# A gated attention unit and its feed-forward layer: staging buffers given to scores, fewer interleaved up groups, respaced score units

## The chip, the cores and the metric

The kernel runs on one core of a Trainium2 chip. A core has five engines with queues of their own: TensorE (PE, matmuls; its weight loads are listed apart as PEld), VectorE (DVE), ScalarE (ACT), GpSimd (POOL) and SyncE (SP, which here only issues transfers). Transfers between main memory and the core's SBUF, and transposing transfers inside SBUF, run on 16 DMA engines; SP, ACT and POOL issue them. Matmul results land in PSUM, eight banks of 128 x 512 f32. The metric is the device time of one execution in microseconds (us); less is better.

## The reference

```python
def _attn_ref(u, v, z):                       # u, v: 8 x 3008 x 256, z: 8 x 3008 x 64
    scores = (1.0 / S) * np.matmul(z, z.transpose(0, 2, 1))
    attn = np.maximum(scores, 0.0) ** 2
    return u * np.matmul(attn, v)

def _moe_ref(x, w_in, w_out):                 # x: 24064 x 256, w_in: 256 x 2048, w_out: 2048 x 256
    h = x @ w_in
    g = h * (1.0 / (1.0 + np.exp(-1.702 * h)))
    return g @ w_out
```

Eight batches of attention with a squared relu in place of a softmax, gated by u, and a feed-forward layer over all rows. The scores are symmetric: the block of rows i and columns j is the transpose of block (j, i).

## The kernel before

**Tiles.** Each batch has 24 row blocks of 128 rows (the last half full) in six chunks of 512 rows (`NCH` = 6, `NJ` = 24). A *score unit* (i, jp) is two row blocks (2jp, 2jp + 1) against chunk i: two score matmuls in 64-row halves of TensorE that run together into a PSUM tile `sc` of two banks (tag "ps2", two tiles, shared with the up-projection's `hg`), a relu by ACT into `rl` (three buffers) and a square by VectorE into `a`. The buffers of tag "a" (21 of them, 2 KB a partition each) hold these units, and also the left sums S1, S2, S4 described below. Because of the symmetry, most units serve a second chunk as well: SP transposes them by a transfer into tiles `tt` (tag "tt", 15 buffers of 4 KB), a tag that the activated tiles `gt` of the feed-forward layer and the staging of the first batch's V and z use too. In batches after the first, the unit on the diagonal is "folded": unit (i, 2i) is computed whole, (i, 2i + 1) only in part, and the rest of it, tile `ad`, comes from a transposing transfer; VectorE writes the other half of `ad`.

**The loop.** The body loops over batches b and chunks i. `attend(b, i)` returns some 47 steps of two matmuls (0.216 us of TensorE each; 0.189 in chunk 5, which is 448 wide) that multiply V by the units into `o` (tag "ps1", four banks). Every engine's order is the order of the program text. Between the steps the loop inserts other work at step numbers written out by hand: score units at the steps in `SCHED0`, `SCHED`, `NEXT` (a dictionary from step to number of units, `take` pops them from a queue in a fixed order), transposes of u (`TURN`), loads (`LOAD`, `LOADW`), and in chunk 4 of a batch (`full(b)`; chunk 5 in the last batch) the *heads*: the first `LAGY` = 18 up groups, spread evenly over the steps. In chunk 5 the inserted units are those of the next batch's chunk 0 (`host` = b + 1); two more are taken at the end of the batch.

**The feed-forward layer.** A batch has 48 up groups q (`up_group`): six blocks k of 512 rows, eight groups each. A group is four matmuls into `hg`, a gelu by ACT into `gf` (two buffers), and a scaled copy to `gt` by VectorE (by ACT where q is at least `LAGY` and q % 4 = 1). The second matmul is done for blocks 0 to 4 (0 to 5 in odd batches) in Strassen's way, with seven products P1 to P7 instead of eight: `left_sums` computes S1 to S4 from a block's `gt` on VectorE, two operations each, and `weight_sums` computes t1 to t4 from W2 once. These operations stand in the list `SUMS`; each up group pops one (two while the list is longer than eight), and a block's eight sums are appended after its last up group. After chunk 5 a loop runs over the remaining up groups, each followed by one product from the list `products`: for k = 0 P1, P6, P5, P7, P2, then for each next k P1(k), P4(k-1), P3(k-1), P6(k), P5(k), P7(k), P2(k), and at the end P4, P3 of the last. Each product is 16 matmuls, 0.89 us. Products that are left behind the last up group are run as `steps`, each of which pops one sum. P6 reads S2 and t2, P5 S1 and t1, P7 S3 and t3, P3 S4, P4 t4. Results go to `y` (tag "y", two buffers) by operations on ACT (`uP`, `y`) and VectorE (`y`), which stand in the engines' queues where their product stands. In even batches block 5 (384 rows) goes through plain matmuls (`down`).

**The first batch's start.** z comes by SP and ACT, is cast by `first_cast` (groups 0 to 3 by VectorE, 4 and 5 by ACT) and transposed by TensorE. V comes in six loads of 512 KB in f32 (`load_v`: two by ACT, four by SP) into staging tiles of tag "tt", and POOL casts each with two copies. In later batches V is loaded by POOL with a cast in the transfer, and z by `load_z` through two staging tiles `zst`.

The lines that the prediction's steps touch: L232 score matmul, L246 and L243 relu, L260, L251 and L244 squares (`a`, half `ad`), L253 and L272 transposing transfers, L332 the attention matmul, L349 to L352 the gate, L373 up matmul, L381 gelu, L383 and L385 `gt`, L420 to L423 weight sums, L441 to L449 left sums, L474 products, L484 to L490 their results.

Of the kernel before, what the change touches and what calls it, by code (L numbers as in the profile page):

```python
# [9 lines left out]
F32 = mybir.dt.float32  # L10
F16 = mybir.dt.float16
P = 128
# [3 lines left out]
def kernel(  # L16
# [13 lines left out]
    AF = mybir.ActivationFunctionType  # L30
    ALU = mybir.AluOpType

    B, S, D = u.shape
    DQK = z.shape[2]
    DFF = moe_w_in.shape[1]

    NJ = (S + P - 1) // P
# [61 lines left out]
    def first_z(n0, n1, eng):  # L99

        if 0 not in ZT:
            ZT[0] = pz.tile([P, NJ, P], F16, name="ZT", tag="ZT")
            ZT["st"] = [pa.tile([P, CB * CB, 2, DQK], F16, name="zst", tag="tt", bufs=15) for _ in range(2)]
            ZT["f"] = [pw.tile([P, CB * CB, DQK], F32, name="zf", tag="y") for _ in range(2)]
        zf = ZT["f"][n0 // (CB * CB)]
        m0 = n0 % (CB * CB)
        t0, last = n0 * P, n1 == NJ
        t1 = (n1 - CB if last else n1) * P
        eng.dma_start(
            zf[:, m0:m0 + (t1 - t0) // P, :].rearrange("p (g n) d -> p g (n d)", n=CB),  # L110
            z[0, t0:t1].rearrange("(g p n) d -> p g (n d)", p=P, n=CB),
        )
        if last:
            m1 = m0 + (t1 - t0) // P
            eng.dma_start(zf[:, m1:m1 + CB - 1, :], z[0, t1:S0].rearrange("(p n) d -> p n d", n=CB - 1))
            for h in range(2):
                eng.dma_start(zf[h * SREM:(h + 1) * SREM, m1 + CB - 1, :], z[0, S0:S])

    def first_cast(g, by_act=False):
        m = g % CB * CB  # L120
        for c in range(2):
            dst, src = ZT["st"][g // CB][:, m:m + CB, c, :], ZT["f"][g // CB][:, m:m + CB, :]
            if by_act:
                act.activation(dst, src, AF.Copy, scale=1.0)
            else:
                dve.tensor_copy(dst, src)

    def first_zt(g):

# [20 lines left out]
    def load_z(b):  # L150
        ZT[b] = pz.tile([P, NJ, P], F16, name="ZT", tag="ZT")
        for n0 in range(0, NJ, NU):
            zst = pu.tile([P, NU, 2, DQK], F16, name="zst", tag="zst")
            full = min(NU, NJ - 1 - n0)
            src = z[b, n0 * P:(n0 + full) * P].rearrange("(n p) d -> p n d", p=P)
            pool.dma_start(zst[:, :full, 0, :], src)
            if full < NU:
                for h in range(2):
                    pool.dma_start(zst[h * SREM:(h + 1) * SREM, full, 0, :], z[b, S0:S])
            pool.tensor_copy(zst[:, :, 1, :], zst[:, :, 0, :])  # L160
            sp.dma_start_transpose(ZT[b][:, n0:n0 + NU], zst.rearrange("p n c d -> p (n c d)"))
# [5 lines left out]
    def load_v(b, n0):  # L167

        if n0 == 0:
            V16[b] = pz.tile([P, NJ, D], F16, name="V16", tag="V16")  # L170
        if b:
            dst, eng = V16[b][:, n0:n0 + VB], pool
        else:
            dst, eng = pa.tile([P, VB, D], F32, name="vst", tag="tt", bufs=15), act if n0 < 2 * VB else sp
        full = min(VB, NJ - 1 - n0)
        eng.dma_start(dst[:, :full, :], v[b, n0 * P:(n0 + full) * P].rearrange("(n p) c -> p n c", p=P))
        if full < VB:
            for h in range(2):
                eng.dma_start(dst[h * SREM:(h + 1) * SREM, full, :], v[b, S0:S])
        if b == 0:  # L180
            for n in range(0, VB, 2):
                pool.tensor_copy(V16[b][:, n0 + n:n0 + n + 2], dst[:, n:n + 2])

# [55 lines left out]
    def square(b, i, jp, sc):  # L239
        rl = pw.tile([P, 2, CH], F16, name="rl", tag="rl", bufs=3)  # L240
        if folded(b, i) and jp == 2 * i + 1:
            rh = rl[:, :, :CH // 2]
            act.activation(rh, sc[:, :, :CH // 2], AF.Relu, scale=csc)  # L243
            dve.tensor_tensor(unit[b, i, jp][:, 1], rh, rh, ALU.mult)  # L244
            return
        act.activation(rl, sc, AF.Relu, scale=csc)  # L246
        if folded(b, i) and jp == 2 * i:
            a = pa.tile([P, CB, 2, P], F16, name="a", tag="a", bufs=21)
            unit[b, i, jp] = a
            r4 = rl.rearrange("p r (q c) -> p r q c", q=CB)  # L250
            dve.tensor_tensor(a.rearrange("p q r c -> p r q c"), r4, r4, ALU.mult)  # L251
            unit[b, i, jp + 1] = pa.tile([P, 2, 2, CH // 2], F16, name="ad", tag="a", bufs=21)
            sp.dma_start_transpose(  # L253
                unit[b, i, jp + 1][:, 0].rearrange("p g (r c) -> p (g r) c", c=P),
                a[:, CB // 2:].rearrange("p q r c -> p (q r c)"),
            )
            return
        a = pa.tile([P, 2, CH], F16, name="a", tag="a", bufs=21)
        unit[b, i, jp] = a
        dve.tensor_tensor(a, rl, rl, ALU.mult)  # L260
        if jp // 2 > i and (turned(b, i) or jp < NU - 2):
            if b and i == 0 and LATE:
                late.append(((jp + 2) % NU, lambda: turn_unit(b, i, jp, a)))
            else:
                turn_unit(b, i, jp, a)

    def turn_unit(b, i, jp, a):
        cj = jp // 2
        if (b, i, cj) not in TT:
            TT[b, i, cj] = pa.tile([P, CB, CB, P], F16, name="tt", tag="tt", bufs=15)  # L270
        k0 = 2 * (jp % 2)
        sp.dma_start_transpose(  # L272
            TT[b, i, cj][:, k0:k0 + 2].rearrange("p r g c -> p (r g) c"),
            a.rearrange("p r c -> p (r c)"),
        )
# [90 lines left out]
    def up_group(b, q):  # L366
        k, fg = divmod(q, NFG)
        i, n = blocks(b)[k]
        hg = ps2.tile([P, FFG, CH], F32, name="hg", tag="ps2")
        for e in range(FFG):  # L370
            ff = fg * FFG + e
            for c in range(NCC):
                pe.matmul(  # L373
                    hg[:, e, :n], W1[:, c, ff * P:(ff + 1) * P], XT[b, i][:, c, :n],
                    start=(c == 0), stop=(c == NCC - 1),
                )
        if fg % 2 == 0:
            GT[b, k, fg // 2] = pa.tile([P, CB, CH], F16, name="gt", tag="tt", bufs=15)
        g = GT[b, k, fg // 2][:, (fg % 2) * FFG:(fg % 2 + 1) * FFG, :n]
        gf = pw.tile([P, FFG, CH], F32, name="gf", tag="gf")  # L380
        act.activation(gf[:, :, :n], hg[:, :, :n], AF.Gelu_apprx_sigmoid, scale=1.0 / FSC)  # L381
        if q >= LAGY and q % 4 == 1:
            act.activation(g, gf[:, :, :n], AF.Copy, scale=FSC)  # L383
        else:
            dve.tensor_scalar(g, gf[:, :, :n], FSC, None, ALU.mult)  # L385
        for s_ in [SUMS.pop(0) for _ in range(min(len(SUMS), 1 + (len(SUMS) > 8)))]:
            s_()
        if k < nst(b) and fg == NFG - 1:
            SUMS.extend(left_sums(b, k) + (weight_sums() if b == k == 0 else []))

# [44 lines left out]
    def left_sum(b, k, name, h):  # L437
        a11, a12, a21, a22 = left(b, k, h, 0), left(b, k, h + 2, 0), left(b, k, h, 1), left(b, k, h + 2, 1)
        if name == "S3":
            ST[b, k, name, h] = a21  # L440
            dve.tensor_tensor(a21, a11, a21, ALU.subtract)  # L441
            return
        s_ = ST[b, k, name, h] = pa.tile([P, CB, 2, P], F16, name="s", tag="a", bufs=21)
        if name == "S1":
            dve.tensor_tensor(s_, a21, a22, ALU.add)  # L445
        elif name == "S2":
            dve.tensor_tensor(s_, ST[b, k, "S1", h], a11, ALU.subtract)  # L447
        else:
            dve.tensor_tensor(s_, a12, ST[b, k, "S2", h], ALU.subtract)  # L449
# [89 lines left out]
        if last:  # L539
            store(b, k, pool)  # L540

    LAGY = 2 * NFG + 2
    HEAD = 2

    def pieces(b, i):
# [6 lines left out]
        k = max(len(lst) - 6, 2)  # L552
        return lst[:k] + lst[-2:] + lst[k:-2]

    NEXT = {n: 1 for n in (3, 8, 13, 17, 31, 36, 41, 46)} | {NJ: 2}
    SCHED = {
        0: {n: 1 for n in (3, 7, 11, 15, 19, 29, 33, 37, 41, 45)} | {NJ: 2},
        1: {n: 1 for n in (2, 7, 12, 17)} | {NJ: 2},
        2: {n: 1 for n in (2, 7, 12, 17)} | {NJ: 2},
        3: {n: 1 for n in (6, 14, 32, 38)} | {NJ: 2},  # L560
        4: {},
# [35 lines left out]
        load_v(0, n0)  # L597
    first_z(2 * CB, 4 * CB, sp)
    first_z(4 * CB, NJ, sp)
    for n0 in range(2 * VB, NJ, VB):  # L600
        load_v(0, n0)
    warm_up(7)
    for g in range(2):
# [14 lines left out]
    for b in range(B):  # L618
# [5 lines left out]
        for i in range(NCH):  # L624
# [4 lines left out]
            for n, step in enumerate(attend(b, i, b == 0 and i < 2)):  # L629
# [2 lines left out]
                if b == 0 and i == 0 and n == 3:  # L632
                    turns[1]()
                if b == 0 and i == 0 and n in FIRST_CAST:
                    first_cast(FIRST_CAST[n], True)
                if b == 0 and i == 0 and n in FIRST_ZT:
                    first_zt(FIRST_ZT[n])()
                if (i, n) in turn:
# [8 lines left out]
                if i == full(b) and n >= HEAD and (n - HEAD) * LAGY // (2 * NJ - 10) >= head and head < LAGY:  # L647
                    up_group(b, head)
                    head += 1
                step()  # L650
        late.sort(key=lambda t: t[0])
        if more:
            for i in range(2):
# [58 lines left out]
```

## Time and profile before

| | us |
|---|---|
| median of six runs | 1203.72 |
| lowest and highest | 1199.45, 1206.33 |
| the profiled execution | 1204.03 |
| its span, first to last instruction | 1202.3 |

| engine | busy us | share |
|---|---|---|
| PE | 1186.3 | 99% |
| ACT | 825.5 | 69% |
| DVE | 823.4 | 68% |
| POOL | 234.6 | 20% |

The profile gives each instruction's start and duration, the idle time of its engine before it, and what ended that idle time (`<-`). Names read out<-in. In the timeline a line is: start, duration (from the first start to the last end of the merged group), engine, line, operation, tiles, shapes, number of instructions, idle time before. In the list of waits it is: total us, times, longest. In the table of stretches: length, then busy us and instructions of PE, PEld, DVE, ACT, POOL, then the granted clock, the share of the 16 DMA engines and GB/s. Matmuls overlap: one of 128 x 512 is listed with some 0.38 us, while the next starts after 0.216. The granted TensorE clock is 0.999 over the span; it is 0.91 in the stretch from 40 to 60 us. A batch takes some 148 us: batch 1 begins at 166.6, its chunk 4 ends near 240, its chunk 5 near 252, and its last product at 315.4.

### The profile page before, as it was taken

The numbers are of one execution on the slowest core, as the hardware profiler recorded it, in microseconds if no ns is written. First come the engines' busy times: TensorE is split into PE (matmuls) and PEld (weight loads), VectorE is DVE, ScalarE is ACT, GpSimd is POOL, SyncE is SP. The second block draws the span as 40 slices with busy tenths as digits, with TensorE's granted clock in tenths as the row PEclk, the third lists the DMA queues.
The fourth block names the chain that finished last, engine by engine and source line by source line (L and its number), as shares of the span: only waits on it lengthen the run. The fifth ranks groups of instructions, "written<-read, shape, count | busy, mean of one in ns | idle before, by whom it ended". The sixth has DMA issues, their size and how long they took to land.

```text
span 1202.3 us, 27542 instructions
## 1 busy us (share of the span) xinstructions
PE 1186.3 (99%) x11427; PEld 724.5 (60%) x11427; DVE 823.4 (68%) x1323; ACT 825.5 (69%) x979; POOL 234.6 (20%) x325
## 2 busy tenths in 40 slices
PE   8999999999999999999999999999999999999998
PEld 3345775467754676546765468554775547855577
DVE  6688855778657775577775777547786577654776
ACT  7787864678656786477864787657776578672785
POOL 5143100331002310123101231013210132101000
PEclk9999999999999999999999999999999999999999
DMA  9996567676587767757778478784688846785012
GB/s 219 178 129 105 130 141 132 90 116 129 122 139 84 119 129 144 128 64 119 133 148 133 57 119 151 146 120 71 98 150 155 117 77 96 163 158 101 1 36 72
DMA packets 373022, 141.81 MB, mean 118 GB/s; under 512 B 315424, under 2 KB 366368, under 8 KB 372896
## 3 DMA queue, kind: packets, MB, share of 16 engines
q1 hardware_dynamic: 314256, 96.77, 44.2%
q0 software_dynamic: 57280, 42.03, 23.7%
q8 instruction: 89, 1.46, 0.5%
q10 hardware_dynamic: 1360, 1.25, 0.3%
q14 instruction: 37, 0.30, 0.1%
HBM read 60.29 MB, written 24.64 MB: 71 GB/s over the span
## 4 chain that ended last, share of the span: by engine, by line
PE 92%; DVE 3%; ACT 3%; DMA 2%; issue 1%; SPq 0%; DVEq 0%; ACTq 0%
PE o L332 36%; PE hg L373 25%; PE st L474 23%; PE sc L232 6%; PE yp L530 2%; ACT rl L246 2%; DVE gt L385 1%; ACT gf L381 1%; DMA tt<-a 1%; DMA zf<-in_z_dram 1%; DMA vst<-in_v_dram 0%; DVE ut L201 0%; DVE s L445 0%; DVE a L260 0%; DVE s L447 0%
## 5 line engine op out<-in xcount | busy, mean ns | idle before, releaser
L381 ACT ACTIVATE gf<-hg 128x1024 f32<-128x1024 f32 (+1 forms) x384 | 385.9, 1005 | 135.1 <-PE hg L373 111.4
L246 ACT ACTIVATE rl<-sc 128x1024 f16<-128x1024 f32 x309 | 304.5, 1025 | 157.8 <-PE sc L232 144.8
L332 PEld LDWEIGHTS <-V 64*128 64x128 f16 (+1 forms) x4052 | 241.0, 95 | 236.8 <-issue 13.6
L373 PE MATMUL hg<-xt,W 128*128 128x512 f16 (+1 forms) x1408 | 354.6, 374 | 0.8 <-ACT gf L381 0.6
L385 DVE TENSOR_SCALAR gt<-gf 128x1024 f16<-128x1024 f32 (+1 forms) x328 | 229.4, 699 | 128.0 <-ACT gf L381 126.6
L332 PE MATMUL o<-a,V 64*128 64x512 f16 (+3 forms) x2286 | 304.2, 369 | 0.0
L260 DVE TENSOR_TENSOR a<-rl 128x1024 f16<-128x1024 f16 x274 | 187.9, 694 | 155.2 <-ACT rl L246 149.7
L194 POOL DMA_DIRECT2D uq<-in_u_dram x188 | 126.7, 681 | 622.0 <-PE sc L232 268.9
L332 PE MATMUL o<-tt,V 64*128 64x512 f16 (+1 forms) x1510 | 237.2, 378 | 2.5 <-DMA tt<-a 2.5
L373 PEld LDWEIGHTS <-W 128*128 128x128 f16 x1536 | 139.9, 98 | 125.2 <-issue 5.8
L474 PEld LDWEIGHTS <-gt 128*128 128x128 f16 x2816 | 169.2, 98 | 30.4
L474 PEld LDWEIGHTS <-s 128*128 128x128 f16 x2112 | 127.2, 98 | 22.8
L232 PE MATMUL sc<-ZT 64*128 64x512 f16 (+1 forms) x688 | 122.0, 367 | 6.9 <-ACT rl L246 6.0
L474 PE MATMUL st<-WT,gt 128*128 128x128 f16 x1408 | 93.0, 219 | 0.0
L474 PE MATMUL st<-W,gt 128*128 128x128 f16 x1408 | 92.3, 219 | 0.0
L474 PE MATMUL st<-WT,s 128*128 128x128 f16 x1408 | 91.0, 219 | 0.0
L490 DVE SCALAR_TENSOR_TENSOR y<-st,uP 128x256 f32<-128x256 f32 x132 | 55.3, 419 | 27.8 <-ACT uP L484 16.5
L484 ACT ACTIVATE uP<-st 128x256 f32<-128x256 f32 x132 | 49.8, 377 | 33.6 <-PE st L474 22.1
L232 PEld LDWEIGHTS <-ZT 64*128 64x128 f16 x688 | 39.3, 94 | 51.1 <-issue 16.1
L349 DVE TENSOR_TENSOR xt<-o,ut 128x512 f16<-128x512 f32 x80 | 51.3, 683 | 22.7 <-PE o L332 22.7
L445 DVE TENSOR_TENSOR s<-gt 128x1024 f16<-128x1024 f16 x88 | 61.1, 709 | 0.0
L449 DVE TENSOR_TENSOR s<-gt,s 128x1024 f16<-128x1024 f16 x88 | 59.6, 681 | 0.0
(51 smaller groups left out, 621.0 us busy)
## 6 DMA issues: line engine op xcount, KB each, us to landing
out_dram<-y SPq DMA_DIRECT2D x40, 512.0 KB, 3.3
uq<-in_u_dram POOLq DMA_DIRECT2D x156, 128.0 KB, 4.2
V<-in_v_dram POOLq DMA_DIRECT2D x35, 256.0 KB, 6.4
tt<-a SPq DMA_TRANSPOSE x232, 3.9
uq<-in_u_dram POOLq DMA_DIRECT2D x32, 112.0 KB, 4.6
vst<-in_v_dram SPq DMA_DIRECT2D x3, 512.0 KB, 5.7
out_dram<-y POOLq DMA_DIRECT2D x4, 384.0 KB, 3.2
zst<-in_z_dram POOLq DMA_DIRECT2D x7, 192.0 KB, 8.0
```

Source lines behind the costliest of these rows:

```text
L194: eng.dma_start(uq[k * QW:(k + 1) * QW, :n // QW].rearrange("t q c k -> t q (c k)"), src[:, :, cs])
L232: pe.matmul(sc[:, r, :m * P], zt[h, 2 * kp + r, :], zt[h, (qi + 1) * CB - m:(qi + 1) * CB, :], start=True, stop=True,)
L246: act.activation(rl, sc, AF.Relu, scale=csc)
L260: dve.tensor_tensor(a, rl, rl, ALU.mult)
L332: ins = pe.matmul(acc[c][:, :n], V16[b][h, j].rearrange("p (c k) -> p k c", k=NCC)[:, c], weights(b, i, j)[h], start=(k, m) == first[c], s ...
L373: pe.matmul(hg[:, e, :n], W1[:, c, ff * P:(ff + 1) * P], XT[b, i][:, c, :n], start=(c == 0), stop=(c == NCC - 1),)
L381: act.activation(gf[:, :, :n], hg[:, :, :n], AF.Gelu_apprx_sigmoid, scale=1.0 / FSC)
L385: dve.tensor_scalar(g, gf[:, :, :n], FSC, None, ALU.mult)
L445: dve.tensor_tensor(s_, a21, a22, ALU.add)
L449: dve.tensor_tensor(s_, a12, ST[b, k, "S2", h], ALU.subtract)
L474: pe.matmul(bank[:, m, :], lhs()[:, f, m, :], right[:, ff, :], start=name in ("P1", "P2", "P5") and m == 0 and ff == 0, stop=ff == NFF // ...
L490: dve.scalar_tensor_tensor(y[:, :, o, c], ST[b, k, "bank" + x], 1.0 / FSC, ST[b, k, "after" + u_], ALU.mult, ALU.add,)
```

## The change

- Buffers: tag "a" 21 to 26, tag "tt" 15 to 14. `load_z` takes its two staging tiles from tag "y" instead of a pool of its own.
- First batch's V: the first three loads (blocks 0 to 11) are staged and cast by POOL as before; the other three are loaded by POOL with a cast in the transfer. Blocks 12 to 15 are issued ahead of blocks 8 to 11.
- `first_cast` always runs on VectorE.
- `LAGY` is 16 instead of 18: 16 heads in chunk 4.
- The steps at which score units are taken: `NEXT` (chunk 5) and `SCHED` for chunks 0 and 1; the numbers of units stay.
- `weight_sums` is put at the front of `SUMS` after chunk 5 of the first batch instead of behind block 0's left sums in chunk 4.

```diff
-            ZT["st"] = [pa.tile([P, CB * CB, 2, DQK], F16, name="zst", tag="tt", bufs=15) for _ in range(2)]
+            ZT["st"] = [pa.tile([P, CB * CB, 2, DQK], F16, name="zst", tag="tt", bufs=14) for _ in range(2)]
...
-    def first_cast(g, by_act=False):
+    def first_cast(g):
         m = g % CB * CB
         for c in range(2):
-            dst, src = ZT["st"][g // CB][:, m:m + CB, c, :], ZT["f"][g // CB][:, m:m + CB, :]
-            if by_act:
-                act.activation(dst, src, AF.Copy, scale=1.0)
-            else:
-                dve.tensor_copy(dst, src)
+            dve.tensor_copy(ZT["st"][g // CB][:, m:m + CB, c, :], ZT["f"][g // CB][:, m:m + CB, :])
...
-            zst = pu.tile([P, NU, 2, DQK], F16, name="zst", tag="zst")
+            zst = pw.tile([P, NU, 2, DQK], F16, name="zst", tag="y")
...
-        if b:
-            dst, eng = V16[b][:, n0:n0 + VB], pool
-        else:
-            dst, eng = pa.tile([P, VB, D], F32, name="vst", tag="tt", bufs=15), act if n0 < 2 * VB else sp
+        by_pool = b == 0 and n0 < 3 * VB
+        dst, eng = V16[b][:, n0:n0 + VB], pool
+        if by_pool:
+            dst, eng = pa.tile([P, VB, D], F32, name="vst", tag="tt", bufs=14), act if n0 < 2 * VB else sp
...
-        if b == 0:
+        if by_pool:
             for n in range(0, VB, 2):
                 pool.tensor_copy(V16[b][:, n0 + n:n0 + n + 2], dst[:, n:n + 2])
...
-        a = pa.tile([P, 2, CH], F16, name="a", tag="a", bufs=21)
+        a = pa.tile([P, 2, CH], F16, name="a", tag="a", bufs=26)
...
-            SUMS.extend(left_sums(b, k) + (weight_sums() if b == k == 0 else []))
+            SUMS.extend(left_sums(b, k))
...
-    LAGY = 2 * NFG + 2
+    LAGY = 2 * NFG
...
-    NEXT = {n: 1 for n in (3, 8, 13, 17, 31, 36, 41, 46)} | {NJ: 2}
+    NEXT = {n: 1 for n in (2, 6, 11, 15, 33, 37, 41, 45)} | {NJ: 2}
     SCHED = {
-        0: {n: 1 for n in (3, 7, 11, 15, 19, 29, 33, 37, 41, 45)} | {NJ: 2},
-        1: {n: 1 for n in (2, 7, 12, 17)} | {NJ: 2},
+        0: {n: 1 for n in (4, 9, 13, 17, 30, 33, 36, 39, 42, 45)} | {NJ: 2},
+        1: {n: 1 for n in (5, 9, 13, 17)} | {NJ: 2},
...
-    for n0 in range(2 * VB, NJ, VB):
+    load_v(0, 3 * VB)
+    load_v(0, 2 * VB)
+    for n0 in (4 * VB, 5 * VB):
         load_v(0, n0)
...
-                    first_cast(FIRST_CAST[n], True)
+                    first_cast(FIRST_CAST[n])
...
+        if b == 0:
+            SUMS[:0] = weight_sums()
         late.sort(key=lambda t: t[0])
```

## The prediction

> **What bounds the kernel now.** I read the page's first lines, then the waits of TensorE, then short stretches of the timeline around each of those waits.
>
> ```profile
> PE 1186.3 (99%) x11427; PEld 724.5 (60%) x11427; DVE 823.4 (68%) x1323; ACT 825.5 (69%) x979; POOL 234.6 (20%) x325
> ...
> PE 92%; DVE 3%; ACT 3%; DMA 2%; issue 1%; SPq 0%; DVEq 0%; ACTq 0%
> ```
>
> TensorE (PE) is busy for 1186.3 of 1202.3 us and holds 92% of the chain that ends last. The change neither adds nor removes a matmul, so only TensorE's waits can move. Its waits, by releaser:
>
> ```profile
> PE sc L232 <- ACT rl L246: 6.0, 13, 0.7
> PE o L332 <- DMA tt<-a: 2.5, 1, 2.5
> ...
> PE hg L373 <- ACT gf L381: 0.6, 2, 0.4
> ```
>
> Thirteen waits of a score matmul, one for a transposing transfer, two in the up-projection. An idle time starts at a modelled matmul end, 0.16 us after the next slot (a 128x512 matmul lasts 0.38 us and the next one starts after 0.216), so each costs 0.16 us more than shown. All that can be won is some 15 us.
>
> **Part 1, five more score buffers (21 to 26).** One of the 13 waits, in batch 1's chunk 5:
>
> ```profile
> 245.82 1.49 PE L332 MATMUL o<-a,V 64*128 64x448 f16 x14
> ...
> 246.47 0.43 DVE L244 TENSOR_TENSOR ad<-rl 128x512 f16<-128x512 f16 x1 [2.32 <-PE o L332]
> ...
> 248.01 0.39 PE L232 MATMUL sc<-ZT 64*128 64x512 f16 x2 [0.70 <-ACT rl L246]
> ```
>
> VectorE sat 2.32 us on tile `ad`, which needs a buffer of tag "a" that chunk 5 still reads; its `rl` buffers and then the score banks fill up behind it. The 14 matmuls are 7 pairs of 0.189 us and end at 247.14; the score starts at 248.01: 0.86 us lost. Count the live "a" tiles at that point: 10 + 2 units that chunk 5 reads, 6 left sums of block 0 and, with 18 heads, 2 of block 1: 20, so (0,0) takes the 21st and `ad` waits. With 16 heads it is 18, and 26 buffers hold all eight that the first score units want before chunk 5's second pass frees some. The wait comes at the same place in batches 1 to 6: **-6 x 0.86 = -5.2**.
>
> **Part 2, respaced units.** The other 7 waits stand at the first unit of chunk 0: score at 317.04 where step 3 would have let it start at 316.62, 0.42 us. One step later (4) it starts from 316.84, so 0.216 is won, seven times: **-1.5**. The new chunk 0 has units three steps apart (0.65 + 0.216 = 0.86 us) where ACT's relus follow each other every 0.91 us (315.96, 316.88, 317.79). Walked through with two banks, and a score waiting for the relu two before it, six such units after the pair at step 24 use up the slack of the six steps before them and no more: 0, at most +0.2 a batch (+1.4).
>
> **Part 3, 16 heads instead of 18.** In chunk 4 a head comes every 2.375 steps instead of 2.11 (38 steps): 0.86 + 0.51 = 1.38 us against 1.32, where VectorE needs two 0.60 us steps for a gt and a left sum. The hg starts lose 0.55 us in batch 0 (two o matmuls at 89.52, the next hg at 90.50 instead of 89.95) and 0.15 to 0.47, 1.5 together, in batches 1 to 6. I take all of the first (the four W2 sums leave too) and 60% of the rest: **-1.4**; between 0 and -2.1.
>
> But two up groups move into the loop behind chunk 5, where each is paired with one product, so two products fewer are left behind the last up group. That matters in batches 1, 3, 5, 7, where block 5 goes through products: its sums can start only after the last gt. Here is VectorE after the last up group of batch 1 (hg from 302.96), all back to back:
>
> ```profile
> 305.44 0.68 DVE L385 TENSOR_SCALAR gt<-gf 128x1024 f16<-128x1024 f32 x1
> ...
> 306.64 0.69 DVE L445 TENSOR_TENSOR s<-gt 128x1024 f16<-128x1024 f16 x1
> ...
> 307.25 0.42 DVE L490 SCALAR_TENSOR_TENSOR y<-st,uP 128x256 f32<-128x256 f32 x1
> 307.58 0.68 DVE L445 TENSOR_TENSOR s<-gt 128x1024 f16<-128x1024 f16 x1
> 308.18 0.42 DVE L490 SCALAR_TENSOR_TENSOR y<-st,uP 128x256 f32<-128x256 f32 x1
> ...
> 308.51 1.28 DVE L447 TENSOR_TENSOR s<-s,gt 128x1024 f16<-128x1024 f16 x2
> ...
> 310.07 1.95 PE L474 MATMUL st<-WT,s 128*128 128x128 f16 x32
> ```
>
> The second S2 is written at 309.79; product P6 of block 5 reads it from 310.07: 0.28 us to spare. With 16 heads the products behind the last hg are P7, P2, P1(5), P4, P3, then P6(5), each 0.89 us: P6 would start at 303.82 + 5 x 0.893 = 308.29. VectorE's queue (steps of 0.60, y 0.33) is gt 305.14 (the gelu ends at 305.11), S4 305.74, y 306.34, y 306.67, S1 307.00 and 307.60, S2 308.20, y of P3 308.80, S2 309.13 to 309.81. P6's first four matmuls wait to 308.95, its next four to about 309.9 instead of 308.51: +1.4. Later the second S4 sits behind y of P7 and y of P2, each waiting for its product, and P3(5) loses another 0.6. What is queued behind the waiting matmul is all of TensorE. **+2.0 x 4 = +8.0**; ends +0.7 (only the first S2 late) and +2.6 a batch.
>
> **Part 4, W2 sums later.** They leave chunk 4 and become the first four sums of batch 0's loop, two a group. P6(0) needs t2 in the second round.
>
> ```profile
> 107.51 1.03 PE L373 MATMUL hg<-xt,W 128*128 128x512 f16 x4
> ...
> 108.37 1.06 PE L474 MATMUL st<-WT,s 128*128 128x128 f16 x16
> ...
> 108.52 0.68 DVE L385 TENSOR_SCALAR gt<-gf 128x1024 f16<-128x1024 f32 x1
> 109.12 0.68 DVE L445 TENSOR_TENSOR s<-gt 128x1024 f16<-128x1024 f16 x1
> ```
>
> VectorE is still at the xt of chunk 5 and starts the first gt at 108.52, when P6 is already running. Behind that gt come t1 and t2, 0.60 each: t2 at 110.4, 0.2 earlier with the last unit one step earlier, against 108.37: **+1.9**. It may also drop the clock: a 0.85 us idle time at 6.8 did not, the 2.46 at 40.8 did (below), at 1.7 us. 1.9 lies nearer the second, but leaves 44% of a 3.41 us stretch busy instead of 28%; I take a quarter, **+0.4**.
>
> **Part 5, V by the POOL queue, casts on VectorE, smaller staging.** Three of six V loads leave SP's queue and their six POOL casts go; POOL issues loads that cast instead, the first behind the cast of V blocks 4 to 7 (about 9.9), the rest near 12.5 and 13.5 to 15. V 12 to 15 is needed at step 24 (16.8), 16 to 19 at 32 (19.7), 20 to 23 at 40 (22.0). POOL's V loads elsewhere land 4.3 to 8.3 us after issue, so about 15, 18 and 20: just in time. The transfer engines are full in this stretch (last columns: granted clock, share of the 16 transfer engines, GB/s):
>
> ```profile
> 0.00:20.00 20.00, 16.95 (x89) 6.44 (x90) 11.43 (x22) 15.30 (x22) 12.95 (x22) 1.00 1.04 259
> 20.00:40.00 20.00, 20.00 (x110) 7.02 (x110) 15.77 (x23) 15.79 (x17) 5.16 (x8) 1.00 1.21 155
> 40.00:60.00 20.00, 17.51 (x147) 8.01 (x144) 11.21 (x18) 13.35 (x15) 3.42 (x6) 0.91 1.11 181
> ```
>
> They move the same V reads, only some 2 us later, and the backlog ends in this wait of chunk 2, for the transpose of unit (1,5):
>
> ```profile
> 43.21 1.31 PE L332 MATMUL o<-tt,V 64*128 64x512 f16 x6 [2.46 <-DMA tt<-a]
> ```
>
> It costs 2.6 us and then eight pairs at half clock (0.43 instead of 0.216), 1.7 more. A backlog 2 us longer makes it 2 us longer: **+2.0**. Ends: -4.3 (SP's queue, free of V, issues transposes sooner and the wait goes) and +5 (see the third rival). The casts: ACT's two of 0.46 become two on VectorE behind the squares that end at 13.52, so the transposes at 13.57 wait some 0.7, and the score at 15.67 no longer loses its 0.5: 0, between -0.7 and +0.7. z staging in "y" buffers and 14 "tt" buffers: 0, for z's last transpose lands at 85.6 and the first y is wanted after 106, and I count at most 13 live "tt" tiles in chunk 4.
>
> The Trainium skill, "SBUF — State Buffer", section "SBUF: two separate sides", speaks against this part: while VectorE runs a two-port operation, POOL cannot write descriptors, and its transfer (0.62 us alone) takes about 3.1. By that each of the three loads would come up to 2.5 us later than I say; POOL's issues here take 0.65 to 0.86 us whatever VectorE does, a few 1.2. On the clock, "TensorE: Matmul & The Clock Gate", "Part 1: The HAM clock gate", asks for an idle window of about 3.4 us before the clock drops; here 2.46 was enough, so for Part 4 the rule would give 0 where I put 0.4.
>
> **Sum:** -5.2 - 1.5 - 1.4 + 8.0 + 1.9 + 0.4 + 2.0 = +4.2. The profiled execution took 1204.03 (span 1202.3, 1.7 around it): 1208.2. It lies 0.3 above the runs' median, so **1208** against 1203.72.
>
> **Rivals.**
> *VectorE's tail stays hidden* (the sums of block 5 are ready in time): the 8.0 go, 1208 - 8 = **1200**, faster. For: the margin of 0.28 shows that the order was once fitted to this. Against: the row above is back to back, and the last gt can't come sooner than its gelu at 305.11. It decides if S2 ends before 308.5.
> *The wait at 40.8 goes:* -4.3 instead of +2.0: **1201.7**, little changed. For: transposes take 5 us to land beside V loads at 10 to 16 and SP loses 6.0 and 5.6 us on two issues between 22 and 36. Against: those two stand beside POOL's u loads, long after V.
> *V comes late in chunk 0:* u loads issued by POOL at 18.5 and 19.2 took 9.1 and 9.8 us to land beside transposes. V 20 to 23 issued at 14.5 would then land at 24.3, 2.3 late or more, and half clock (1.7): **1212**. It takes the place of part of the wait at 40.8.
>
> **How the numbers follow.** Chances: forecast 0.40 (1204.5 to 1211 by its own bounds), tail hidden 0.22, wait gone 0.18, V late 0.20. About 0.3%, 3.6 us, is what a measurement can tell: below 1200.1 is faster, above 1207.3 slower. Slower: 0.26 of the forecast's 0.40, all of V late: 0.46. Faster: 0.13 of the hidden tail, 0.06 of the wait gone: 0.19. The rest, 0.35, within. Range 1199 to 1213, from just below the hidden tail to just above V late.
>
> **What would show it.** The chunk 5 waits near 248, 397, 543, 691, 838, 986 gone; those at the batch starts halved; a new wait of TensorE L474 for VectorE s in the tails of batches 1, 3, 5, 7 (some 1.4 and 0.6), and one for WT near 108; the wait for tt near 40 longer, none on V. If no L474 wait appears, the largest term is wrong.

## The result and the profile after

| | before | after |
|---|---|---|
| median us | 1203.06 (37 runs, 1199.45 to 1209.71) | 1208.67 (16 runs, 1205.10 to 1211.65) |
| ratio, 95% interval | | 1.0044 [1.003, 1.0058] |
| profiled execution us | 1204.03 | 1207.36 |
| its span us | 1202.3 | 1205.6 |

The kernel after is slower by some 5 us: 0.44% of 1203 by the ratio, 5.6 between the medians. Line numbers of the changed kernel lie up to 4 lower from the middle of the file on: its score matmul is L228, the attention matmul L328, the product L470, S2 is L443, S4 L445, t2 is written by L417.

The first lines of the page after, and of its chain the shares by engine:

```profile
PE 1187.7 (99%) x11427; PEld 722.8 (60%) x11427; DVE 818.3 (68%) x1319; ACT 830.1 (69%) x983; POOL 227.9 (19%) x324
...
PE 93%; DVE 3%; ACT 2%; DMA 1%; issue 1%; SPq 0%; DVEq 0%; ACTq 0%
```

Nothing has changed in kind: the same 11427 matmuls fill 99% of the span. So the 3.3 us between the two spans must again be time in which TensorE waits or runs at half clock. The list of its waits after (total us, times, longest):

```profile
PE st L470 <- DVE s L443: 4.2, 8, 0.5
PE sc L228 <- ACT rl L242: 3.5, 1, 3.5
PE st L470 <- DVE WT L417: 2.0, 1, 2.0
PE st L470 <- DVE s L445: 1.8, 4, 0.5
```

Of the thirteen waits of a score only one is left, at another place (below). The wait for a transposing transfer (2.5) is not there. New are twelve waits of products for left sums, three in each of four batches, and one for t2.

For the account I took for every matmul the time from its predecessor's start to its own, less what the predecessor's size asks for (0.216 us for 512 columns), and summed the excess by place in both traces:

| TensorE time lost, us | before | after | difference |
|---|---|---|---|
| score units in chunk 5, batches 1 to 6 | 5.19 | 0 | -5.19 |
| first score unit of a batch | 2.91 | 1.40 | -1.51 |
| up matmuls (hg) in chunk 4 | 2.07 | 0 | -2.07 |
| tail, products for S2 and S4 | 0 | 7.96 | +7.96 |
| product for t2 in batch 0 | 0 | 2.15 | +2.15 |
| the first 62 us | 12.63 | 14.53 | +1.90 |
| the rest | 12.05 | 12.46 | +0.41 |

That makes 34.85 against 38.50, +3.65, where the spans differ by 3.3. The largest term is the tail, the products that run behind the last up group of a batch. The timeline of batch 1 there, kernel after:

```profile
309.30 0.69 DVE L381 TENSOR_SCALAR gt<-gf 128x1024 f16<-128x1024 f32 x1
309.90 0.68 DVE L445 TENSOR_TENSOR s<-gt,s 128x1024 f16<-128x1024 f16 x1
310.51 0.75 DVE L486 SCALAR_TENSOR_TENSOR y<-st,uP 128x256 f32<-128x256 f32 x2
...
311.17 1.28 DVE L441 TENSOR_TENSOR s<-gt 128x1024 f16<-128x1024 f16 x2
...
312.37 0.68 DVE L443 TENSOR_TENSOR s<-s,gt 128x1024 f16<-128x1024 f16 x1
312.98 0.42 DVE L486 SCALAR_TENSOR_TENSOR y<-st,uP 128x256 f32<-128x256 f32 x1
...
313.11 0.40 PE L470 MATMUL st<-WT,s 128*128 128x128 f16 x4 [0.50 <-DVE s L443]
313.31 0.68 DVE L443 TENSOR_TENSOR s<-s,gt 128x1024 f16<-128x1024 f16 x1
...
314.05 1.74 PE L470 MATMUL st<-WT,s 128*128 128x128 f16 x28 [0.54 <-DVE s L443]
...
319.14 0.84 PE L470 MATMUL st<-W,s 128*128 128x128 f16 x12 [0.46 <-DVE s L445]
```

VectorE works from 309.30 without a gap: gt, S4, two y, S1 twice, S2, y, S2. P6 of block 5 could have started at 312.4 and waits for the first S2 till 313.11, for the second till 314.05; P3 waits for the second S4 till 319.14. Three waits (0.50, 0.54 and 0.46 idle after the modelled end; 0.67, 0.70 and 0.62 against the next slot), and the same three from 608, 903 and 1195 on.

### The profile page after: what moved, and what is told of

The parts are those of the page before. It is cut to its first block, busy times and chain, and to the rows that moved or that the text cites. A ratio compares the mean times of both kernels' runs of the same rounds, so it can differ in the third digit from the quotient of the medians.

```text
span 1205.6 us, 27542 instructions
## 1 busy us (share of the span) xinstructions
PE 1187.7 (99%) x11427; PEld 722.8 (60%) x11427; DVE 818.3 (68%) x1319; ACT 830.1 (69%) x983; POOL 227.9 (19%) x324
## 4 chain that ended last, share of the span: by engine, by line
PE 93%; DVE 3%; ACT 2%; DMA 1%; issue 1%; SPq 0%; DVEq 0%; ACTq 0%
PE o L328 39%; PE hg L369 26%; PE st L470 20%; PE sc L228 6%; PE yp L526 2%; DMA uq<-in_u_dram 1%; ACT gf L377 1%; DVE s L445 1%; DVE y L486 1%; DVE gt L381 1%; DVE s L441 0%; DVE s L443 0%; PE w L97 0%; ACT rl L242 0%; ACT uP L480 0%
## 5 line engine op out<-in xcount | busy, mean ns | idle before, releaser
L328 PEld LDWEIGHTS <-V 64*128 64x128 f16 (+1 forms) x4052 | 240.0, 95 | 236.2 <-issue 14.3
L381 DVE TENSOR_SCALAR gt<-gf 128x1024 f16<-128x1024 f32 (+1 forms) x320 | 222.2, 694 | 146.8 <-ACT gf L377 143.4
L328 PE MATMUL o<-a,V 64*128 64x512 f16 (+3 forms) x2286 | 305.2, 369 | 0.0
L328 PE MATMUL o<-tt,V 64*128 64x512 f16 (+1 forms) x1510 | 234.4, 377 | 0.0
L470 PEld LDWEIGHTS <-gt 128*128 128x128 f16 x2816 | 169.5, 98 | 31.8
L470 PEld LDWEIGHTS <-s 128*128 128x128 f16 x2112 | 127.8, 98 | 35.4 <-DVE s L443 5.5
L228 PE MATMUL sc<-ZT 64*128 64x512 f16 (+1 forms) x688 | 122.0, 368 | 4.3 <-ACT rl L242 3.5
L470 PE MATMUL st<-WT,s 128*128 128x128 f16 x1408 | 93.1, 219 | 6.1 <-DVE s L443 4.2
L470 PE MATMUL st<-WT,gt 128*128 128x128 f16 x1408 | 93.0, 219 | 0.0
L470 PE MATMUL st<-W,gt 128*128 128x128 f16 x1408 | 92.3, 219 | 0.0
L228 PEld LDWEIGHTS <-ZT 64*128 64x128 f16 x688 | 39.0, 94 | 48.6 <-issue 13.6
L379 ACT ACTIVATE gt<-gf 128x1024 f16<-128x1024 f32 (+1 forms) x64 | 66.0, 1031 | 2.0
L197 DVE STREAM_TRANSPOSE ut<-uq 128x1024 f32<-128x1024 f32 (+1 forms) x48 | 58.2, 1213 | 5.7 <-DMA uq<-in_u_dram 5.7
```

Source lines behind the costliest of these rows:

```text
L197: dve.transpose(ut[:, :, :n // QW, :].rearrange("p k q t -> p q k t"), UQ.pop((b, i))[:, :n // QW].rearrange("p q c k -> p q k c"),)
L228: pe.matmul(sc[:, r, :m * P], zt[h, 2 * kp + r, :], zt[h, (qi + 1) * CB - m:(qi + 1) * CB, :], start=True, stop=True,)
L328: ins = pe.matmul(acc[c][:, :n], V16[b][h, j].rearrange("p (c k) -> p k c", k=NCC)[:, c], weights(b, i, j)[h], start=(k, m) == first[c], s ...
L470: pe.matmul(bank[:, m, :], lhs()[:, f, m, :], right[:, ff, :], start=name in ("P1", "P2", "P5") and m == 0 and ff == 0, stop=ff == NFF // ...
```

## The experiments

"Before" in the measured ratios is the kernel before, run on the same chip between the others. Only the differing lines are shown.

**The heads alone, and the buffers alone.** The kernel before with 16 heads (`before_16_heads`), and the kernel before with the new staging and buffers (`before_buffers`):

```diff
-    LAGY = 2 * NFG + 2
+    LAGY = 2 * NFG
```

```diff
-            zst = pu.tile([P, NU, 2, DQK], F16, name="zst", tag="zst")
+            zst = pw.tile([P, NU, 2, DQK], F16, name="zst", tag="y")
...
-        a = pa.tile([P, 2, CH], F16, name="a", tag="a", bufs=21)
+        a = pa.tile([P, 2, CH], F16, name="a", tag="a", bufs=26)
```

(and 14 for 15 at tag "tt".)

> The kernel before with 16 heads and nothing else. Theory (two products fewer behind the last up group make block 5's sums late): waits of TensorE L474 for VectorE s of 0.67, 0.70 and 0.62 us in the tails of batches 1, 3, 5, 7, +8.0; the hg waits of chunk 4 (2.1) nearly gone, -1.9; and, since only 18 'a' tiles are then live at the start of chunk 5, the third unit and not the second meets the full ring, the three rl buffers cover it, and most of the 0.86 us waits go without any further buffer, -4 to -5.2. Sum 1203 + 8.0 - 1.9 - 4.6 = 1204.5. Rival (the tail's waits come from the other order of work in the changed kernel, not from the heads): no tail waits, 1196.5.

> The kernel before with the buffers alone: 26 'a', 14 'tt', z staged in 'y'; 18 heads, old steps, old V. Theory: the six chunk 5 waits go (-5.2), batch starts (0.42 x 7) and the wait for tt near 40 stay, no tail waits: 1203 - 5.2 = 1198. Rival (18 heads on 14 'tt' buffers make gt or a transpose wait): new waits in chunk 4 or the products, 1203 or more.

Heads alone: 1202.76 (12 runs), ratio 1.0005 [0.9985, 1.0026]. The waits of TensorE in this kernel (the product is L474 here, S2 L447):

```profile
PE st L474 <- DVE s L447: 4.5, 8, 0.8
PE sc L232 <- ACT rl L246: 3.1, 8, 1.4
PE st L474 <- DVE s L449: 1.8, 4, 0.5
```

The twelve waits of the tail are there, again 0.67, 0.70 and 0.62 (once 0.95 in place of 0.67), with nothing else of the change: the tail is the price of the heads. But the waits in chunk 5 of batches 1 to 6 are gone too, with 21 buffers, as was expected: with two up groups fewer in chunk 4 there are fewer left sums that hold a buffer. Seven of the eight score waits left are those of the batch starts; the eighth is taken up below.

Buffers alone: 1199.11 (12 runs), ratio 0.9972 [0.9952, 0.9993]: the chunk 5 waits are gone, no tail wait is there, the batch starts keep their 0.42. The interval lies below 1, so the gain is real. In batch 0 of this execution VectorE comes to the W2 sums before their load has landed (94.3):

```profile
DVE WT L421 <- DMA W<-in_moe_w_out_dram: 2.0, 1, 2.0
DVE WT L420 <- DMA W<-in_moe_w_out_dram: 1.9, 1, 1.9
```

Behind it a score of chunk 5 of batch 0 loses 3.4 us at 101. The buffers need not be the cause: with 21 of them `before_16_heads` has the same two waits (1.2 and 1.4) and loses 1.5 us at 96, its eighth score wait. The profiled execution of the kernel before lost more in its first 62 us and came to these sums 2 to 3 us later, when the loads were there. So either edit alone removes the waits in chunk 5, and doing both buys nothing more there.

**18 heads again, and the tail's order mended.** The kernel after with `LAGY` back at 18 (`after_18_heads`, the diff above turned round), and the kernel after with 16 heads, block 5's P2 moved ahead of its P6 and two sums instead of one for each product behind the last up group (`after_tail_mended`):

```diff
+            if k == NCH - 1:
+                one = one[-1:] + one[:-1]
...
-            if SUMS:
-                SUMS.pop(0)()
+            for s_ in [SUMS.pop(0) for _ in range(min(len(SUMS), 2))]:
+                s_()
```

> The changed kernel with 18 heads again. Theory: the tail waits go (-8.0), the hg waits of chunk 4 come back in part (+1 to +2), the chunk 5 waits stay away: 1208.7 - 8.0 + 1.5 = 1202. The wait for W2's sums (2.1) stays, since the loop still starts with them. Rival (the tail's lateness comes from the sums' place in the queue, whatever the number of heads): 1208.7, waits at L470 unchanged.

> The changed kernel with 16 heads, but in odd batches product P2 of block 5 goes ahead of its P6, and the steps behind the last up group pop two sums each. Theory: of the 2.0 us a batch some 0.1 to 0.4 is left: 1208.7 - 7 = 1201.7. Rival (VectorE's chain from the last gelu sets it, whatever the order): the wait moves to P6 or P3 with 1 us or more a batch, 1205 or more.

18 heads: 1202.69 (12 runs), ratio 0.9987 [0.9971, 1.0003]. No tail wait is left, the up matmuls of chunk 4 lose 1.6 us again (2.07 before), and the kernel is 0.0057 (some 7 us) below the kernel after, by intervals that do not touch. The tail's order mended: 1205.61 (12 runs), ratio 1.0007 [0.9984, 1.003]. The tail goes from 2.0 to 0.8 us a batch, not to the 0.1 to 0.4 expected. VectorE's part of it is down to 0.16, one wait for S2. The other 0.64 is new, and in batch 1 it stands here (L482 is in this kernel ACT's copy of a result out of PSUM):

```profile
318.25 1.06 PE L472 MATMUL st<-WT,gt 128*128 128x128 f16 x16
319.35 0.38 ACT L482 ACTIVATE uP<-st 128x256 f32<-128x256 f32 x1 [1.40 <-PE st L472]
319.78 1.05 PE L472 MATMUL st<-WT,gt 128*128 128x128 f16 x16 [0.47 <-ACT uP L482]
```

The first line is block 5's P7, the last its P4. In `product` P6, P7 and P4 all add to the PSUM bank that P1 began, and ACT copies that bank out behind P7. ACT's copy starts as soon as P7 has ended; P4 may not add to the bank before the copy is done. In the old order P2 ran between P7 and P4 and covered the copy. Moving P2 ahead took that cover away: 60% of the tail's loss is gone, and what is left is mostly the price of the new order.

**The W2 sums spread over chunk 5.** The kernel after, with t1 to t4 computed at four steps of batch 0's chunk 5:

```diff
-        if b == 0:
-            SUMS[:0] = weight_sums()
...
+                if b == 0 and i == NCH - 1 and n == 0:
+                    wsums = weight_sums()
+                if b == 0 and i == NCH - 1 and n in (10, 14, 20, 29):
+                    wsums.pop(0)()
```

> The changed kernel with the four W2 sums given to VectorE one by one at steps 10, 14, 20 and 29 of the first batch's chunk 5. Theory: the wait of TensorE L470 for WT near 110 (2.15 us, and half clock behind it in some executions) goes, the tail waits stay: 1208.7 - 2.2 = 1206.5, down to 1205.5 where the half clock counted. Rival (VectorE is full there too, so the squares of chunk 5 come late instead): no gain, a wait at L228 or L369 near 100.

1206.50 (12 runs), ratio 1.0013 [0.9993, 1.0033]. The wait for t2 is gone, no other stands between 96 and 120, and the tail's waits are unchanged. The two profiled spans differ by 0.8 us only, since this execution loses 15.9 in its first 62 us. The medians differ by 2.2 us, the ratios by 0.0031; their intervals just overlap, so the gain rests on the trace more than on the times.

**V as before, u earlier, u by SP.** Three kernels on the first 62 us, each the kernel after but for one thing. `after_v_staged` loads all of the first V by ACT and SP and casts it on POOL, as before; the casts of z stay on VectorE. `after_u_first` has SP issue u of chunk 0 ahead of the transposes. `after_u_by_sp` has SP, not POOL, issue u of the first batch's later chunks:

```diff
-        by_pool = b == 0 and n0 < 3 * VB
+        by_pool = b == 0
...
-    load_v(0, 3 * VB)
-    load_v(0, 2 * VB)
-    for n0 in (4 * VB, 5 * VB):
+    for n0 in range(2 * VB, NJ, VB):
```

```diff
     load_v(0, 2 * VB)
+    load_u(0, 0)
...
-                if b == 0 and i == 0 and n == 5:
-                    load_u(0, 0)
```

```diff
-        eng = pool if b or i else sp
+        eng = pool if b else sp
```

> The changed kernel with all six V loads staged and cast by POOL as before. Theory (V's loads from POOL's queue hold up the u of chunk 0, which SP issues beside them, and VectorE waits for it): the wait of 3.7 us near 31 and the half clock behind it go, the transpose wait near 41 comes back in some executions: 1208.7 - 2 to - 6, centre 1204.5. Rival (the transfers are full either way and u is late with any order): the same start, 1208.7.

> The changed kernel with the four loads of chunk 0's u issued by SP right behind V blocks 8 to 11, ahead of the first transposes. Theory: u lands near 15 instead of 28, the wait near 31 goes; V or a transpose may be late by 0 to 2 us instead: 1208.7 - 4, 1204.7. Rival (the same bytes in a full stretch, so that another wait of the same size takes its place, V at step 32 or 40): 1208 or more.

> The kernel after, with u of the first batch's chunks 1 to 5 issued by SP instead of POOL; nothing else is changed. In the kernel after, POOL has no cast to do behind its V loads and so issues u of chunk 1 at 14.5 to 16.5, some 2.6 us earlier than before; these land at 22.8 to 25.9, ahead of SP's u of chunk 0 (issued 14.8 to 17.4, landing 25.4 to 28.1), for which VectorE and then TensorE wait (3.7 us at 31.2, and half clock behind it). Theory: it is these loads of u that stand in the way, not the V loads by POOL. Then u of chunk 0 lands by about 22 to 24, the wait at 31 is gone, the start loses 9 to 11 us instead of 14.5, and the time is some 4.5 us below the kernel after: about 1204, ratio to the kernel before about 1.000. Rival: the V loads that POOL casts in the transfer are what fills the DMA engines, whoever issues u: u of chunk 0 still lands after 25, the start loses 13 us or more, the ratio stays at 1.003 to 1.005, 1207 to 1209.

What they start from is this stretch of the kernel after (timeline):

```profile
28.20 1.25 DVE L197 STREAM_TRANSPOSE ut<-uq 128x1024 f32<-128x1024 f32 x1 [5.66 <-DMA uq<-in_u_dram]
...
30.12 1.94 ACT L242 ACTIVATE rl<-sc 128x1024 f16<-128x1024 f32 x2 [3.78 <-DVE a L256]
...
31.19 0.40 PE L228 MATMUL sc<-ZT 64*128 64x512 f16 x2 [3.55 <-ACT rl L242]
...
31.52 2.74 PE L328 MATMUL o<-a,V 128*128 128x512 f16 x6
```

VectorE's transpose of u waits 5.66 us for its load, the squares and relus behind it are late, and TensorE waits 3.55 (3.72 against the next slot). Then six matmuls take 2.74, some 0.43 each instead of 0.216. The four loads of u that it waits for were issued at 14.8 to 17.4 and landed at 25.4 to 28.1, 10.5 us each; before, issued at 14.5 to 16.2, they landed at 17.8 to 20.0.

V staged: 1205.23 (12 runs), ratio 1.0002 [0.9985, 1.0019], clear of the kernel after's interval. u lands at 18.3 to 21.8, VectorE does not wait for it, and the start loses 10.35 us instead of 14.53. One wait of 1.34 at 16.1 is left, for z's cast on VectorE.

u first: 1209.15 (11 runs, 1202.51 to 1216.34; a twelfth took 1220.67), ratio 1.0040 [1.0015, 1.0066]. u lands at 11 to 13 and the wait at 31 is gone, as that theory had it, but the median is no lower. The wait list of the profiled execution (1212.30) and the matmuls behind the wait:

```profile
PE o L328 <- DMA tt<-a: 8.2, 1, 8.2
...
PE o L328 <- DMA V<-in_v_dram: 1.1, 2, 0.9
```

```profile
50.43 1.46 PE L328 MATMUL o<-tt,V 64*128 64x512 f16 x6 [8.23 <-DMA tt<-a]
```

V is now 1 us late, and a transposing transfer of chunk 2 by 8.2 us. By the median the rival held: another wait took the place of the first. It does not do so in every execution: four of the runs (1202.5 to 1204.8) lie below every run of the kernel after, the other seven at 1208 and more. No trace shows one of the four.

u by SP: 1206.03 (12 runs), ratio 1.0009 [0.9994, 1.0024]. The ratio lies between the theory's 1.000 and the rival's 1.003, nearer the first, and clear of the kernel after's interval. The reason holds only in part: TensorE still waits, 2.56 us instead of 3.72, and the start loses 12.6. I had overlooked that the text issues chunk 1's u first, so that on one queue chunk 0's stands behind it and behind a transpose that took 4.5 us to issue. It is issued 4 to 5 us later (19.9 to 21.6), and yet lands sooner (24.4 to 26.2): 4.6 us after issue instead of 10.5. That speaks for POOL's u loads as the larger part of the lateness; what POOL's V loads add, this run does not separate.

**The parts that pay, together.** 26 buffers, the new staging and steps, but 18 heads, V and z's casts as before, and the W2 sums in chunk 5: `combined`, and once more as `combined_again` beside two variants, one with the first batch's u by SP, one with the casts on VectorE. The edits are those shown, and for the last one the change's own `first_cast`.

> What the runs so far speak for: 26 'a' buffers, new steps, 18 heads, V and casts as before the change, W2 sums in chunk 5. Theory: no tail waits, no chunk 5 waits, batch starts 0.2, hg waits 1.5 to 2 in all, start as before: before_buffers' 1199.1 less 1.5 (batch starts) less 1 to 3 (the W2 sums' wait for their load in chunk 4): 1196. Rival (the new steps need 16 heads): new waits in chunk 5 or 0, 1199 or more.

> The combined kernel once more, as the base of the two beside it: 1192 to 1199, median 1194.5; the spread comes from the wait for a transpose near 44, which its first profile shows with 4.2 us and which other executions lack.

> The combined kernel with the first batch's u issued by SP alone instead of POOL. Theory (loads from POOL's queue beside transposes are what makes the engines slow between 17 and 42 us): the wait for tt near 44 goes in all executions, 1192.5, with a smaller spread. Rival (the same bytes are moved in the same stretch; and SP's transposes now stand behind u loads that wait for a free buffer): no gain or a longer wait, 1195 or more.

> The combined kernel with first_cast on VectorE, as the change has it. Theory (both waits weigh the same: 0.5 at the score behind ACT's copies against 0.7 at the transposes behind VectorE's casts): within 1 us of the combined kernel. Rival (ACT was the start's limit and VectorE has room): 1 us or more faster; or, since the cast stands behind two squares, up to 1.3 slower, as the wait of 1.3 us near 16 in after_v_staged suggests.

| | median us (runs) | ratio to before |
|---|---|---|
| combined | 1194.36 (7) | 0.9933 [0.9906, 0.9959] |
| combined_again | 1193.91 (6) | 0.9917 [0.9887, 0.9948] |
| combined_u_by_sp | 1193.76 (6) | 0.9910 [0.9884, 0.9936] |
| combined_casts_dve | 1195.01 (7) | 0.9926 [0.9900, 0.9953] |

All four beat both kernels. The first two came out 1.6 and 0.6 us below what was expected, u by SP 1.3 above. The waits of TensorE that `combined_again` has left:

```profile
PE w L97 <- DVE nil L75: 1.2, 1, 1.2
PE hg L373 <- ACT gf L381: 0.9, 4, 0.3
PE sc L232 <- ACT ZT L141: 0.8, 3, 0.4
PE zp L133 <- DVE zst L126: 0.7, 2, 0.4
```

Lost in all 24.3 us, against 34.8 before and 38.5 after; half of that is spread over single matmuls. Neither variant can be told from it by its median. u by SP has the smallest spread (1192.88 to 1194.37, six runs), and its trace shows a possible reason: from 23.8 to 33.4 SP's transposes are issued every 1.4 us and land within 3.5 of it, where with POOL's loads beside them one issue takes 6.2 us (`combined_again`). With casts on VectorE a 1.5 us wait for z is back at 14.8, and that execution also has the wait for a transpose, 2.4 at 43.8.

## Why the prediction was right

The time, 1208.0, and its sign came out: 1208.67 by the median, 1207.36 in the profiled execution. The terms for the buffers, the respaced units, the heads and the tail came out by the mechanisms that the prediction gave; the term for the start came out by luck.

- **Buffers, -5.2:** -5.19 in the trace, all six waits gone. Buffers alone gave 0.9972, -3.4 us, and lost 3.4 in batch 0 at the W2 load. The prediction counted 18 tiles with 16 heads, but did not conclude that 16 heads would then do without the new buffers, as `before_16_heads` shows: the gain here is not the buffers' alone.
- **Respaced units, -1.5:** -1.51. The chunk 0 units three steps apart cost nothing, as walked through.
- **Heads, -1.4:** -2.07, its own lower end: all the waits of hg went.
- **Tail, +8.0:** +7.96. The three waits came where they were put; the 1.4 for S2 measured 0.67 + 0.70, the 0.6 for S4 0.62. The rival that the tail stays hidden fell with the trace; `before_16_heads`, which has these waits without the rest of the change, and `after_18_heads`, which has the rest without these waits, put them down to the heads.
- **W2 sums, +1.9 and +0.4:** 2.15, without half clock in the profiled execution. Of the six profiled kernels with this wait three show half clock behind it: in `after_18_heads` 1.98 us of idle time is followed by the up matmuls below, four in 1.91 us where they take 1.03 in the kernel after. Three of six, at 1.7 each, would be a mean of 0.85: +0.4 was the right kind of term, and probably too small.

```profile
112.66 1.28 PE L470 MATMUL st<-WT,s 128*128 128x128 f16 x16 [1.98 <-DVE WT L417]
113.74 1.91 PE L369 MATMUL hg<-xt,W 128*128 128x512 f16 x4
```

- **V by POOL, +2.0:** +1.90 between the two traces, but this is the step that failed, and the match is luck: "A backlog 2 us longer makes it 2 us longer", of the wait at 40.8. That wait vanished, as in the second rival, yet without its gain. V came as estimated (14.8, 18.1 and 20.1 to 21.5 against "about 15, 18 and 20") with no wait on it. Late was u of chunk 0, which the prediction did not follow, though SP issues it in that stretch; and POOL, free of its casts, issues u of chunk 1 at 14.5 instead of 17.1, ahead of it.
- **What the +1.90 is made of:** +4.8 from 28 to 37 us (the wait for u and half clock behind it), +1.4 from 7 to 13 (a stretch of half clock from 7.6 on, ahead of any V load by POOL, which the profiled execution of the kernel before lacks), -3.9 from 42 to 48 (the wait for the transpose), and -0.4 elsewhere. The size is also larger than the two traces show. The five executions with V, u and z's casts as before lose 8.3, 8.3, 9.3, 12.6 and 13.9 us in the first 62, the four with V, u and the casts as in the kernel after 14.5 to 15.9, and putting V back gave 0.0042, 5 us. The profiled execution of the kernel before had the wait for the transpose, which three of these five have not.

The other terms add up to +1.3 in the trace (-5.19 - 1.51 - 2.07 + 7.96 + 2.15); with some 5 for the start that is 6.3, against 5.6 between the medians. So the forecast came this near partly because errors cancel: half clock behind t2 and the start were put low, and the heads' gain was put low too. The profiled execution of the kernel after also shows less half clock than most: its mean granted clock is 0.997, where nine of the 16 runs have 0.995 or 0.996.

## What to carry to other kernels

Work taken out of a filled stage must be followed to where it lands: two up groups fewer in chunk 4 removed 2 us of waits there and, by themselves, 5 in chunk 5, and brought 8 back at the batches' ends, where the products that had hidden VectorE's sums were missing. An order that is changed to hide one wait can uncover another: look at what each moved piece stood between, as P2 stood between P7 and P4. An edit that frees an engine's queue lets what stands behind it start sooner: list what each queue issues next, and who else is loading then. Where the transfers are full, a new order can move the wait, and by how much differs between executions: `after_u_first` ranged over 14 us.

## What the runs showed of the hardware

- **Half clock in stretches of 3.41 us.** In all 14 traces, every stretch of half clock on record, but for those at the very end, is 3.4 or 6.8 us long. A wait of 1.98 us was followed by one in `after_18_heads` and by none in the kernel after: the same idle time, another outcome.
- **Executions differ with it.** Of 94 runs of the kernel before beside the experiments, the 31 with a mean granted clock of 1.000 have a median of 1200.8 us, the 20 with 0.997 one of 1207.2, and on each of the four chips used the two groups lie 5.7 to 7.1 apart. A mean of 0.997 is some 3.6 us of full clock less (0.003 x 1203), about two stretches at 1.7 each; an estimate for the rest, 2.8, is waits, but these runs have no traces. The median of the kernel before (1202.1 to 1206.1 in the five groups of runs) thus also says how often that happens.
- **Mixed transfers.** SP's four loads of u for chunk 0 took 3.3 to 3.8 us from issue to landing in the kernel before, 10.5 to 10.7 beside POOL's loads in the kernel after, 4.6 to 4.7 with all of u on SP's queue. The issue of a transpose on SP took 1.3 us each from 23.8 to 33.4 in `combined_u_by_sp`, where POOL loads nothing; beside POOL's loads single ones took 6.2 (`combined_again`) and 8.1 (`after_u_first`).
